# A fused attention and expert kernel: the first head's maxima moved ahead, and three smaller moves

## The chip, the cores and the metric
One core of a Trainium2 chip runs the whole program in one launch. The core has five engines that each work through their own list of instructions in order: TensorE (PE; its weight loads are shown as PEld), VectorE (DVE), ScalarE (ACT), GpSimd (POOL) and SyncE (SP), which here only starts transfers. ACT starts some transfers too, from the same list as its arithmetic. The metric is the device time of one execution in microseconds (us). Before the change it is 790.23 us, the median of three runs (789.36 to 791.34).

## The reference
Three steps follow each other. Only the first is touched by most of the change.

```python
# clustered attention: 2 batches x 8 heads, 768 tokens, head size 64, 16 centroids per head
q_assign = argmax(q_n @ c_n); k_assign = argmax(k_n @ c_n)         # rows normalised
mask   = q_assign[..., :, None] == k_assign[..., None, :]
scores = where(mask, q @ k.T / 8, -1e9); scores -= max(scores, -1)
attn   = exp(scores); attn /= sum(attn, -1) + 1e-9
x = (attn @ v) laid out as 1536 tokens x 512
# dense layer: 512 -> 2048 -> 512, weights arrive as 64-bit floats
x = (s * relu(x @ w_in) ** 2 + b) @ w_out
# 8 experts, top 1: logits from the rows of x and of expert_emb, both normalised
logits = xn @ en.T / tau; e = argmax(logits)
out = softmax(logits)[e] * (relu(x @ w1[e]) @ w2[e])
```

## The kernel before
The attention handles 16 heads one after the other, and the work of neighbouring heads is interleaved. A list of entries `(time, function)` is filled with `at(t, f)` and sorted by time; the functions are called in that order, and `order.pin` fixes each engine's list to it. A head is 12 units of this time long: head j starts at `o = 12 * j`, and the table `TIMES` gives each step's place against `o`. The numbers are only an order, not microseconds; in the steady part a head takes about 15 us.

For one head the steps are these. `load` fetches q, k and v. `split` cuts q and k into a rounded high part (ACT) and a rest (POOL; DVE for head 0). `trans` transposes them, three blocks of 128 columns at a time, in four calls: k first half, k second half, q first half, q second half. Each goes to a PSUM bank and ACT copies it to `kb` or `qb`; for all heads but the first, all four use the one bank `t`, so a transpose waits for the copy before it. `sims_mm` multiplies with the centroids; `sims_a` to `sims_e` and `masks`, all on DVE, turn that into one-hot rows scaled by 2^33, which are laid under the high parts of q and k in `qa` and `ka`. For heads 0 and 1 four copies do this, two on ACT and two on DVE; later heads use transfers. `M` then gives masked scores for 128 queries by 384 keys, and DVE takes their row maximum; there are 12 such pairs per head. `mneg` joins the maxima and negates them, `mrow` turns them into a row (a small matmul `mr`, an ACT copy `mrs`, a transfer into row 96 of `qa`). `Sx` computes the scores transposed, with the mask and the maximum already in the product, and ACT takes the exponential into `pt`; there are 12 per head too, in the two banks `s0` and `s1`. `V` multiplies `pt` with v into the bank `pv`, in three pairs of two (units 5.45, 9.45 and 13.45). `pv_out` reads that bank on ACT with two instructions, `vm` and `xu`, and the next head's first `V` may write it only after that. `sums` and `norm_a` to `norm_c` divide by the sums of the exponentials.

Head j's maxima and head j+2's or j+3's transposes stand among head j's neighbours' scores. Before head 0's first `Sx`, nothing but such preparation can run: heads 0 to 2 are split, transposed and masked there, and head 0's and half of head 1's maxima are taken. `cst.heat` issues matmuls on constant data whose result is not used; two follow each of head 0's 12 `M`. Head 0's `M` rotate over five PSUM banks, those of later heads over `M0` and `M1`.

`Moe.hooks` puts steps of the later layers into the same list. `fetch` and the last of nine steps of `conv_steps` start two transfers of 512 KB each on ACT's queue, for a raw weight tile pair (six buffers); the other eight steps convert an earlier pair from 64-bit floats, on ACT and DVE. `length`, `unit` and `project` prepare the expert embeddings: ACT sums squares, `unit` is eight DVE instructions, `project` is four transposes into bank `t` and one DVE instruction. They are used first in the routing after the dense layer's first 512 tokens.

Of the kernel before, what the change touches and what calls it, by code (L numbers as in the profile page):

```python
# [9 lines left out]
F32 = mybir.dt.float32  # L10
# [5 lines left out]
AF = mybir.ActivationFunctionType  # L16
# [5 lines left out]
P = 128  # L22
# [3 lines left out]
HS = S // 2  # L26
# [2 lines left out]
MASK = float(2 ** 33)  # L29
GUARD = 1e-9  # L30
TIMES = dict(load=-49, loadv=-18, split=(-42, -40), trans=(-36.6, -35.6, -33.6, -32.6), sims=-30.53, simv=(-26.5, -26.5, -26.5, -22.52, -22.52, -22.51),
             M=-17.4, mneg=-5.7, mrow=-3.5, V=(5.45, 5.45, 9.45, 9.45, 13.45, 13.45), presum=3.0, norm=(14.5, 25.47, 29.5, 29.5, 29.5))
ENDS = {14: (14.5, 21.47, 22.4, 23.4, 24.4), 15: (14.5, 14.6, 14.7, 14.8, 14.9)}
WARM = -26
HEAT = ((-41, 7), (-30.5, 6), (-22, 6))
SETUP, FETCH = 6.3, (5.3, 17.3, 29.3)
CONV = (3.2, 5.2, 7.2, 11.2, 15.2, 19.2, 23.2, 27.2, 31.2)
F, DM, TC = 2048, 512, 512
NF, KD, NTT = F // P, DM // P, TC // P
E, F2 = 8, 1024  # L40
# [51 lines left out]


def attention(ax, tc, cst, q, k, v, cen, xt, hooks, embed):
    nc = tc.nc
    ident, identr, ones, desc, cc, ps = cst.ident, cst.identr, cst.ones64, cst.desc, cst.cc, cst.ps
    io = ax.enter_context(tc.tile_pool(name="io", bufs=3))
    w1 = ax.enter_context(tc.tile_pool(name="w1", bufs=2))
# [5 lines left out]
    qa = [ab.tile([P, S], F32R, name=f"qa{i}") for i in range(NSET)]  # L104
    ka = [ab.tile([P, S], F32R, name=f"ka{i}") for i in range(NSET)]
# [66 lines left out]
    si, sm = {}, {}  # L172
# [31 lines left out]

    def masks(j):
        i = j % NSET
        ot = w1.tile([P, HS], F32, name="ot", tag="ot")
        nc.vector.transpose(out=ot, in_=si.pop(j))
        for g in range(4):
            da, w = (qa, ka)[g // 2][i], slice(g % 2 * HS, (g % 2 + 1) * HS)  # L210
            if j >= NSET:
                nc.sync.dma_start(out=da[64:64 + NC_, w].bitcast(F32), in_=ot[32 * g:32 * g + NC_])
            elif j > 1:
                nc.sync.dma_start(out=da[64:96, w].bitcast(F32), in_=ot[32 * g:32 * g + 32])
            elif g % 2 == 0:
                nc.scalar.activation(out=da[64:96, w], in_=ot[32 * g:32 * g + 32], func=AF.Copy)
            else:
                nc.vector.tensor_copy(da[64:96, w], ot[32 * g:32 * g + 32])

    def M(j, r, c):  # L220
        i = j % NSET
        pp = ps([P, HS], "M", f"M{c}" if j else ("M0", "M1", "s0", "s1", "s2")[(2 * r + c) % 5])
        nc.tensor.matmul(pp, qa[i][0:80, r * P:(r + 1) * P], ka[i][0:80, c * HS:(c + 1) * HS])  # L223
        nc.vector.tensor_reduce(out=mxt[j % 2][:, r, c:c + 1], in_=pp, axis=AX.X, op=ALU.max)  # L224
# [90 lines left out]
    c = w1.tile([P, D], F32, name="c", tag="c")  # L315
# [21 lines left out]
    def at(t, f, *a):  # L337
        ops.append((t, len(ops), f, a))
# [8 lines left out]
    T = TIMES  # L347
    for j in range(NH):
        o = 12 * j
        if j >= 3:  # L350
            at(o + T["load"], load, j, "qk")
            at(o + T["loadv"], load, j, "v")
        if j > 0:
            for i in range(2):
                at(o + T["split"][i], split, j, i)
        for i in range(4):
            at(o + T["trans"][i], trans, j, "kq"[i // 2], i % 2)
        at(o + T["sims"], sims_mm, j)
        for i, f in enumerate((sims_a, sims_b, sims_c, sims_d, sims_e, masks)):
            at(o + T["simv"][i], f, j)  # L360
        for r in range(NR):
            for c in range(2):
                at(o + T["M"] + 2 * r + c, M, j, r, c)
                if j == 0:
                    at(o + T["M"] + 2 * r + c, cst.heat, 2, "pv")
        at(o + T["mneg"], mneg, j)
        at(o + T["mrow"] if j else -5.6, mrow, j)
        for t in range(NR):
            for c in range(2):
                at(o + 2 * t + c, Sx, j, t, c)  # L370
            at(o + T["V"][t], V, j, t)
            at(o + 2 * t + T["presum"], presum, j, t)
        for i, f in enumerate((pv_out, sums, norm_a, norm_b, norm_c)):
            at(o + ENDS.get(j, T["norm"])[i], f, j)
# [6 lines left out]
class Moe:  # L381
# [11 lines left out]
    def hooks(self, ms, mb):  # L393
        nc = self.nc

        def early():
            for i, t in enumerate((ms, mb)):
                nc.sync.dma_start(out=self.sb[:, i:i + 1], in_=t.rearrange("(o n) -> o n", o=1).to_broadcast([P, 1]))
            self.setup()

        def fetch(f):
            self.loaded[f] = self.load_f64(f, nc.scalar)

        self.loaded, self.wT, self.wraw, self.running = {}, {}, {}, {}
        out = [(-27, self.length), (SETUP, early), (-16.6, self.unit), (SETUP + 9, self.project)] + [(t, lambda f=f: fetch(f)) for f, t in enumerate(FETCH)]
        for f in range(NWA):
            for n, t in enumerate(CONV):
                out.append((36 * f + 16 + t if f < NWA - 1 else 176.2 + n, lambda f=f: next(self.steps(f), None)))
        return out
# [50 lines left out]
    def ps(self, shape, name, tag):  # L460
        return self.cst.ps(shape, name, dict(a="pv", b="sm", y0="t", y1="s0", y2="s1", y3="s2").get(tag, tag))
# [124 lines left out]
    def moe1(self, xt):  # L586
# [4 lines left out]
        for c in range(self.chunks):  # L591
# [4 lines left out]
            def up(f):  # L596
# [4 lines left out]
                if final:  # L601
                    self.load_expert(f + 1)
                    if f in PRE0:
                        z = PRE0.index(f)
                        with self.after(*tail):
                            self.pre0[z] = self.half(self.wraw[0, z], 0, nc.gpsimd, False)
                hp = self.ps([P, TC], "hp", f"M{f % 2}")
                self.up_mm(hp, *wu, lambda k: x[k // 2][:, k % 2], lambda k: x[2 + k // 2][:, k % 2])
# [431 lines left out]
    def prep(self, xr):  # L1040
# [12 lines left out]
        return xh, xl  # L1053

    def block(self, y, args, w, pre, hooks, wd=None, g0=None):
        nc = self.nc
        xh, xl, off, _ = args
# [5 lines left out]
        def up(f):  # L1063
            with ExitStack() as behind:
# [5 lines left out]
                if f not in wd:  # L1070
                    wd[f] = self.half(w[f], 1, nc.vector)
            hp = self.ps([P, T], "hp", f"M{f % 2}")
            if xl is None:
# [79 lines left out]
@with_exitstack  # L1153
def tile_kernel(ctx, tc, q, k, v, cen, w_in, w_out, ms, mb, emb, tau, w1, w2, out):
    nc = tc.nc
    cst = consts(ctx, tc)
    xp = ctx.enter_context(tc.tile_pool(name="xp", bufs=1))
    xt = [xp.tile([P, KD, TC], F32, name="xt", tag=f"xt{i}") for i in range(NT // TC)]
    sb = cst.pool.tile([P, 2], F32, name="sb")
    moe = Moe(ctx, tc, cst, w_in, w_out, sb, emb, tau, w1, w2, out)  # L1160

    with ExitStack() as ax:
        attention(ax, tc, cst, q, k, v, cen, xt, moe.hooks(ms, mb), moe.embed)
    moe.pools()
    moe.xp = xp
    moe.moe1(xt)
    moe.spare = [xp.tile([P, KD, TC], dt, name="spare", tag=f"xt{i}") for i, dt in enumerate((F32R, F32R, F32))]
    moe.experts()
# [26 lines left out]
```

## Time and profile before

| | before |
|---|---|
| median of three runs | 790.23 us |
| profiled execution, its own time | 785.38 us |
| its span, first to last instruction | 783.5 us |
| mean granted TensorE clock | 0.987 of full |
| PE busy | 747.7 us, 95% |
| DVE busy | 518.4 us, 66% |
| ACT busy | 423.3 us, 54% |
| POOL busy | 352.1 us, 45% |

The profiled execution is one of many and has its own time, 4.85 us below the median; 1.88 us of it lie outside the span. Busy times are sums over the span. PE is busy nearly throughout, so what counts is where it is not, and whether its work there is of use: the matmuls of `heat` count as busy.

### The profile page before, as it was taken

What the parts mean: (1) busy time and instruction counts of PE and PEld (TensorE: products, weight loads), DVE (VectorE), ACT (ScalarE), POOL (GpSimd) and SP (SyncE); (2) the same over time, 40 slices, a digit from 0 to 9 for tenths busy, and PEclk for the clock granted to TensorE, in tenths of its full rate; (3) what the DMA queues carried; (4) which work ended last, traced back from release to release, by engine and by line L of the source; (5) the groups of instructions that cost most, each with busy time, mean ns of one, the idle gap of its engine ahead of it and who ended that gap; (6) DMA issues with size and microseconds to landing.
All of it is one profiled execution on the core that took longest, in us unless ns stands there. A gap on an engine that the chain in (4) does not pass through costs nothing. (4 is left out here: it accounts for less than half of the span.)

```text
span 783.5 us, 12256 instructions
## 1 busy us (share of the span) xinstructions
PE 747.7 (95%) x4193; PEld 564.0 (72%) x4193; DVE 518.4 (66%) x1100; ACT 423.3 (54%) x843; POOL 352.1 (45%) x282
## 2 busy tenths in 40 slices
PE   7799999999999899999999999999999999999993
PEld 3465555565555468888787887877879998988983
DVE  5768989797997889984354442557567365755750
ACT  5266555655554576555445564454557365755650
POOL 3166776676685565445333544467132302230001
PEclk9899999999999999999999999999999999999997
DMA  5145443434322225511000042265235555865600
GB/s 154 42 129 176 107 124 81 140 87 135 79 64 80 69 61 171 161 55 54 1 1 1 1 161 82 81 215 167 80 117 177 184 192 179 250 215 195 220 17 24
DMA packets 75678, 88.72 MB, mean 113 GB/s; under 512 B 7526, under 2 KB 58630, under 8 KB 75345
## 3 DMA queue, kind: packets, MB, share of 16 engines
q1 hardware_dynamic: 66688, 66.52, 28.1%
q0 software_dynamic: 4208, 13.90, 5.5%
q10 hardware_dynamic: 4704, 7.34, 2.8%
q8 instruction: 40, 0.66, 0.3%
q14 instruction: 38, 0.30, 0.1%
HBM read 70.57 MB, written 7.34 MB: 99 GB/s over the span
## 5 line engine op out<-in xcount | busy, mean ns | idle before, releaser
L534 POOL TENSOR_TENSOR wl<-w,wh 128x512 fp32r<-128x512 f32 x96 | 123.0, 1306 | 128.8 <-ACT wh L532 126.1
L249 ACT ACTIVATE pt<-S 128x384 f32<-128x384 f32 x192 | 91.8, 489 | 101.1 <-PE S L248 98.8
L224 DVE TENSOR_REDUCE mx<-M 128x1 f32<-128x384 f32 x192 | 101.9, 552 | 37.1 <-PE M L223 34.6
L260 POOL TENSOR_TENSOR acc<-acc,pt 128x768 f32<-128x768 f32 x61 | 106.0, 1737 | 5.7 <-ACT pt L249 3.3
L555 PE MATMUL hp<-x,wh 128*128 128x512 f32 x384 | 105.1, 395 | 0.3 <-ACT wh L532 0.3
L555 PE MATMUL hp<-x,spare 128*128 128x256 f32 x732 | 96.0, 284 | 2.0 <-PEq L987 1.7
L555 PEld LDWEIGHTS hp<-x,spare 128*128 128x128 f32 x732 | 92.6, 190 | 6.9 <-issue 4.1
L563 PE MATMUL y<-wd,gg 128*128 128x512 f32 x360 | 93.2, 394 | 0.0
L611 DVE SCALAR_TENSOR_TENSOR hp<-hp,sb,t 128x512 f32<-128x512 f32 x48 | 36.4, 758 | 74.6 <-ACT t L610 74.6
L223 PE MATMUL M<-ka,qa 80*128 80x384 f32 x192 | 79.0, 412 | 4.2 <-DVE mx L224 3.1
L555 PEld LDWEIGHTS hp<-x,wh 128*128 128x128 f32 x384 | 70.6, 188 | 15.1 <-ACT wh L532 0.9
L563 PE MATMUL y<-wh,gh 128*128 128x512 f32 x192 | 74.9, 390 | 0.0
L563 PE MATMUL y<-wl,gh 128*128 128x512 f32 x192 | 74.7, 389 | 0.0
L247 PE MATMUL S<-qa,ka 97*128 97x384 f32 x192 | 71.0, 370 | 2.1 <-ACT pt L249 1.4
L268 PE MATMUL pv<-pt,vn 128*64 128x385 f32 x384 | 72.8, 500 | 0.0
L548 DVE TENSOR_TENSOR wd<-w,wd 128x512 fp32r<-128x512 f32 x64 | 43.3, 686 | 44.1 <-ACT wd L547 43.3
L563 PEld LDWEIGHTS y<-wd,gg 128*128 128x128 f32 x360 | 63.8, 189 | 9.9
L1036 POOL DMA_INDIRECT row<-rows,idx x24 | 27.9, 1163 | 88.0 <-PE tp L1048 49.1
L248 PE MATMUL S<-qb,kb 128*128 128x384 f32 x192 | 65.5, 341 | 0.0
L610 ACT ACTIVATE t<-hp 128x512 f32<-128x512 f32 x48 | 28.7, 598 | 67.6 <-PE hp L555 67.5
L223 PEld LDWEIGHTS M<-ka,qa 80*128 80x128 f32 x192 | 36.9, 192 | 38.2 <-DVE su L296 8.1
L532 ACT ACTIVATE wh<-w 128x1024 fp32r<-128x1024 f32 x48 | 50.4, 1055 | 17.7 <-PE y L563 12.9
(275 smaller groups left out, 1352.2 us busy)
## 6 DMA issues: line engine op xcount, KB each, us to landing
w<-in_moe_w_dram SPq DMA_DIRECT2D x128, 256.0 KB
raw<-in_moe_w_in_dram SPq DMA_DIRECT2D x9, 512.0 KB
raw<-in_moe_w_out_dram SPq DMA_DIRECT2D x9, 512.0 KB
raw<-in_moe_w_in_dram ACTq DMA_DIRECT2D x7, 512.0 KB
raw<-in_moe_w_out_dram ACTq DMA_DIRECT2D x7, 512.0 KB
qn<-in_q_dram SPq DMA_DIRECT2D x16, 192.0 KB
kn<-in_k_dram SPq DMA_DIRECT2D x16, 192.0 KB
vn<-in_v_dram SPq DMA_DIRECT2D x16, 192.0 KB
```

Source lines behind the costliest of these rows:

```text
L223: nc.tensor.matmul(pp, qa[i][0:80, r * P:(r + 1) * P], ka[i][0:80, c * HS:(c + 1) * HS])
L224: nc.vector.tensor_reduce(out=mxt[j % 2][:, r, c:c + 1], in_=pp, axis=AX.X, op=ALU.max)
L247: nc.tensor.matmul(pp, ka[i][0:97, t * P:(t + 1) * P], qa[i][0:97, w], start=True, stop=False)
L248: nc.tensor.matmul(pp, kb[i][:, t * P:(t + 1) * P], qb[i][:, w], start=False, stop=True)
L249: exps.setdefault((j, t), []).append(nc.scalar.activation(out=p[:, c, 0:HS], in_=pp, func=AF.Exp, scale=0.125).ins)
L260: eng.tensor_tensor(out=acc[j][-1], in0=acc[j][-1], in1=p[:, :, 0:HS], op=ALU.add)
L268: together(tc, [lambda c=c: nc.tensor.matmul(pv_t[j][c * 64:c * 64 + 64, :], io_t["v", j][:, t, :], p[:, c, :], start=t == 0, stop=t == NR ...
L532: nc.scalar.activation(out=wh, in_=w, func=AF.Copy)
L534: eng.tensor_tensor(out=wl[:, a], in0=w[:, a], in1=wh[:, a].bitcast(F32), op=ALU.subtract)
L548: eng.tensor_tensor(out=t[:, 1], in0=w[:, a], in1=t[:, 0].bitcast(F32), op=ALU.subtract)
L555: self.nc.tensor.matmul(hp, a[:, k * P:(k + 1) * P], b(k), start=n == 0, stop=n == 3 * KD - 1)
L563: self.nc.tensor.matmul(y[i], (gl if n == 2 else gh)[:, s], wl if n == 1 else wh, start=first and n == 0, stop=last and n == 2)
```

## The change
Four things move. The diff is shown whole but for context.

```diff
-             M=-17.4, mneg=-5.7, mrow=-3.5, V=(...), presum=3.0, norm=(14.5, 25.47, 29.5, 29.5, 29.5))
+             M=(-17.4, 1), mneg=-5.7, mrow=-3.5, V=(...), presum=3.0, norm=(15.45, 25.47, 29.5, 29.5, 29.5))
-CONV = (3.2, 5.2, 7.2, 11.2, 15.2, 19.2, 23.2, 27.2, 31.2)
+CONV = (3.2, 5.2, 7.2, 11.2, 15.2, 19.2, 23.2, 27.2, 29.48)
     def masks(j):
-        ot = w1.tile([P, HS], F32, name="ot", tag="ot")
+        ot = sm[j] = w1.tile([P, HS], F32, name="ot", tag="ot")
...
-            elif g % 2 == 0:
-                nc.scalar.activation(out=da[64:96, w], in_=ot[32 * g:32 * g + 32], func=AF.Copy)
-            else:
+            elif g % 2:
                 nc.vector.tensor_copy(da[64:96, w], ot[32 * g:32 * g + 32])
+    def copies(j):
+        for g in (0, 2):
+            nc.scalar.activation(out=(qa, ka)[g // 2][j][64:96, 0:HS], in_=sm[j][32 * g:32 * g + 32], func=AF.Copy)
...
+        if j < 2:
+            at((-22.5, -8.5)[j], copies, j)
         for r in range(NR):
             for c in range(2):
-                at(o + T["M"] + 2 * r + c, M, j, r, c)
+                first, step = T["M"] if j else (-20.7, 0.95)
+                at(o + first + step * (2 * r + c), M, j, r, c)
                 if j == 0:
-                    at(o + T["M"] + 2 * r + c, cst.heat, 2, "pv")
-        at(o + T["mneg"], mneg, j)
-        at(o + T["mrow"] if j else -5.6, mrow, j)
+                    at(o + first + step * (2 * r + c), cst.heat, 1, "pv")
+        at(o + T["mneg"] if j else -9.9, mneg, j)
+        at(o + T["mrow"] if j else -9.8, mrow, j)
...
-        out = [(-27, self.length), (SETUP, early), (-16.6, self.unit), (SETUP + 9, self.project)] + [...]
+        out = [(-27, self.length), (SETUP, early), (49.5, self.unit), (53.4, self.project)] + [...]
```

The first place is PE's list where head 0's maxima begin. Here `qs` are head 1's q parts, `qb_117` and `kb_121` head 1's transposed q and k, `qa_108` and `ka_112` head 0's operands; `work` is what `heat` multiplies. Before:

```order
L162 MATMUL tp<-identr,qs 128x128 x6
L178 MATMUL si<-qb_117,cc 32x384 x2
L178 MATMUL si<-kb_121,cc 32x384 x2
L223 MATMUL M<-ka_112,qa_108 128x384
L1133 LDWEIGHTS work
L1133 MATMUL heat<-work 128x512
L1133 LDWEIGHTS work
L1133 MATMUL heat<-work 128x512
```

And the same place in the list of the changed kernel:

```order
L162 MATMUL tp<-identr,qs 128x128 x3
L225 MATMUL M<-ka_112,qa_108 128x384
L1138 LDWEIGHTS work
L1138 MATMUL heat<-work 128x512
L162 MATMUL tp<-identr,qs 128x128 x3
L225 MATMUL M<-ka_112,qa_108 128x384
L1138 LDWEIGHTS work
L1138 MATMUL heat<-work 128x512
L225 MATMUL M<-ka_112,qa_108 128x384
L1138 LDWEIGHTS work
L1138 MATMUL heat<-work 128x512
L178 MATMUL si<-qb_117,cc 32x384 x2
```

Three of the twelve maxima now stand ahead of head 1's products with the centroids, one of them between the two halves of head 1's q transposes, and one `heat` matmul follows each instead of two.

The second place is the end of head 0's maxima on PE, where its row `mr` is made. `qb_118` and `kb_122` are head 2's, `qa_109` and `ka_113` head 1's. Before, and behind it the changed list:

```order
L178 MATMUL si<-qb_118,cc 32x384 x2
L178 MATMUL si<-kb_122,cc 32x384 x2
L223 MATMUL M<-ka_112,qa_108 128x384
L1133 LDWEIGHTS work
L1133 MATMUL heat<-work 128x512
L1133 LDWEIGHTS work
L1133 MATMUL heat<-work 128x512
L235 MATMUL mr<-identr,mn 6x128
L223 MATMUL M<-ka_113,qa_109 128x384 x5
L162 MATMUL tp<-identr,ks 128x128 x3
```

```order
L225 MATMUL M<-ka_112,qa_108 128x384
L1138 LDWEIGHTS work
L1138 MATMUL heat<-work 128x512
L237 MATMUL mr<-identr,mn 6x128
L162 MATMUL tp<-identr,qs 128x128 x6
L178 MATMUL si<-qb_118,cc 32x384 x2
L178 MATMUL si<-kb_122,cc 32x384 x2
L225 MATMUL M<-ka_113,qa_109 128x384 x5
L162 MATMUL tp<-identr,ks 128x128 x3
```

The whole of head 2's q transposes and its products with the centroids moved from ahead of `mr` to behind it. On ACT the copies of head 1's masks moved too, from ahead of head 2's two `qb` copies to behind them; head 0's mask copies stand in ACT's list where they stood.

The third place is ACT's list in head 3, with that head's `pv_out` of head 2 (`vm`, `xu`) and the two weight transfers. Before, then changed:

```order
L168 ACTIVATE qb_118<-tp 128x384
L276 ACTIVATE vm<-pv 128x1
L277 ACTIVATE xu<-pv,vm 128x384
L249 ACTIVATE pt_127<-S 128x384
L168 ACTIVATE qb_118<-tp 128x384
L249 ACTIVATE pt_128<-S 128x384 x2
...
L249 ACTIVATE pt_131<-S 128x384 x2
L525 DMA raw<-in_moe_w_in_dram 128x4x256
L526 DMA raw<-in_moe_w_out_dram 128x1024
L168 ACTIVATE kb_123<-tp 128x384
```

```order
L168 ACTIVATE qb_118<-tp 128x384
L251 ACTIVATE pt_127<-S 128x384
L168 ACTIVATE qb_118<-tp 128x384
L278 ACTIVATE vm<-pv 128x1
L279 ACTIVATE xu<-pv,vm 128x384
L251 ACTIVATE pt_128<-S 128x384 x2
...
L530 DMA raw<-in_moe_w_in_dram 128x4x256
L531 DMA raw<-in_moe_w_out_dram 128x1024
L251 ACTIVATE pt_131<-S 128x384 x2
L168 ACTIVATE kb_123<-tp 128x384
```

`vm` and `xu` moved behind one exponential and the second `qb` copy, in this and every head that has them; the transfers moved ahead of two exponentials, four times in the attention.

## Rows read from the trace of the kernel before
**Rows 1.** Stretches: bounds, length, busy us (instructions) by engine, granted clock, DMA share, GB/s.
```profile
13.00:16.00 3.00, 1.52 (x13) 0.67 (x14) 0.00 (x0) 2.25 (x5) 0.51 (x1) 1.00 0.29 65
16.00:20.00 4.00, 4.00 (x13) 1.82 (x12) 3.48 (x13) 0.00 (x0) 1.44 (x2) 0.57 0.51 148
36.00:40.00 4.00, 3.48 (x13) 3.29 (x14) 2.77 (x7) 1.36 (x3) 0.00 (x0) 0.58 0.04 11
```
**Rows 2.** Timeline before head 0's scores: start, us, engine, line, operation [idle before <-releaser].
```profile
12.81 0.52 ACT L216 ACTIVATE ka<-ot 32x384 fp32r<-32x384 f32 x1
13.89 0.44 PE L162 MATMUL tp<-identr,qs 128*128 128x128 f32 x3 [1.09 <-ACT qb L168]
15.70 0.44 PE L223 MATMUL M<-ka,qa 80*128 80x384 f32 x1
16.25 0.56 DVE L224 TENSOR_REDUCE mx<-M 128x1 f32<-128x384 f32 x1 [3.25 <-PE M L223]
19.36 0.58 DVE L184 STREAM_TRANSPOSE si<-si 128x384 f32<-128x384 f32 x1
21.44 1.94 DVE L224 TENSOR_REDUCE mx<-M 128x1 f32<-128x384 f32 x4
23.30 0.36 DVE L199 TENSOR_TENSOR si<-si,smx 128x192 f32<-128x192 f32 x1
25.45 1.02 DVE L224 TENSOR_REDUCE mx<-M 128x1 f32<-128x384 f32 x2
26.32 0.57 PE L162 MATMUL tp<-identr,qs 128*128 128x128 f32 x3 [2.09 <-ACT qb L168]
29.35 0.73 PE L178 MATMUL si<-qb,cc 128*32 128x384 f32 x2
30.34 0.44 PE L223 MATMUL M<-ka,qa 80*128 80x384 f32 x1
31.41 0.17 DVE L230 TENSOR_REDUCE mn<-mx 128x6 fp32r<-128x18 f32 x1
31.74 0.59 PE L223 MATMUL M<-ka,qa 80*128 80x384 f32 x2
36.90 0.53 PE L247 MATMUL S<-qa,ka 97*128 97x384 f32 x1
```
**Rows 3.** Timeline of PE and ACT around one head's `pv_out`.
```profile
86.41 0.18 ACT L276 ACTIVATE vm<-pv 128x1 f32<-128x1 f32 x1
86.58 0.45 PE L162 MATMUL tp<-identr,qs 128*128 128x128 f32 x3 [0.20 <-ACT vm L276]
86.62 0.58 ACT L277 ACTIVATE xu<-pv,vm 128x384 f32<-128x384 f32 x1
87.10 0.49 ACT L249 ACTIVATE pt<-S 128x384 f32<-128x384 f32 x1
87.64 0.44 PE L247 MATMUL S<-qa,ka 97*128 97x384 f32 x1
88.18 1.51 PE L268 MATMUL pv<-pt,vn 128*64 128x385 f32 x8
```
**Rows 4.** Timeline of PE and ACT where weight transfers are started.
```profile
141.73 0.96 ACT L249 ACTIVATE pt<-S 128x384 f32<-128x384 f32 x2 [1.55 <-PE S L248]
142.74 0.46 ACTq L526 DMA_DIRECT2D raw<-in_moe_w_out_dram  x1
143.79 0.45 PE L162 MATMUL tp<-identr,ks 128*128 128x128 f32 x3 [0.48 <-ACT kb L168]
```
**Rows 5.** Timeline of ACT: `vm` in three other heads.
```profile
55.40 0.18 ACT L276 ACTIVATE vm<-pv 128x1 f32<-128x1 f32 x1
71.23 0.18 ACT L276 ACTIVATE vm<-pv 128x1 f32<-128x1 f32 x1
102.30 0.18 ACT L276 ACTIVATE vm<-pv 128x1 f32<-128x1 f32 x1
```
**Rows 6.** Timeline of PE: a late head without transposes.
```profile
240.78 0.45 PE L247 MATMUL S<-qa,ka 97*128 97x384 f32 x1 [0.25 <-ACT pt L249]
```

More of the change, by code (lines that the diff above doesn't have):

```diff
@@ L31 @@
 TIMES = dict(load=-49, loadv=-18, split=(-42, -40), trans=(-36.6, -35.6, -33.6, -32.6), sims=-30.53, simv=(-26.5, -26.5, -26.5, -22.52, -22.52, -22.51),
-             M=-17.4, mneg=-5.7, mrow=-3.5, V=(5.45, 5.45, 9.45, 9.45, 13.45, 13.45), presum=3.0, norm=(14.5, 25.47, 29.5, 29.5, 29.5))
+             M=(-17.4, 1), mneg=-5.7, mrow=-3.5, V=(5.45, 5.45, 9.45, 9.45, 13.45, 13.45), presum=3.0, norm=(15.45, 25.47, 29.5, 29.5, 29.5))
 ENDS = {14: (14.5, 21.47, 22.4, 23.4, 24.4), 15: (14.5, 14.6, 14.7, 14.8, 14.9)}
@@ L404, in hooks @@
         self.loaded, self.wT, self.wraw, self.running = {}, {}, {}, {}
-        out = [(-27, self.length), (SETUP, early), (-16.6, self.unit), (SETUP + 9, self.project)] + [(t, lambda f=f: fetch(f)) for f, t in enumerate(FETCH)]
+        out = [(-27, self.length), (SETUP, early), (49.5, self.unit), (53.4, self.project)] + [(t, lambda f=f: fetch(f)) for f, t in enumerate(FETCH)]
         for f in range(NWA):
```

## Prediction
> **What bounds the kernel now.** I read the page's busy times first: PE is busy for 95% of the span, so a change pays only where PE waits or does work that is not needed. Then the timeline of the first 37 us. There the reader should see that PE's share is high only because of the idle matmuls of `heat`, and that the work which must be done is a chain over DVE: head 0's twelve maxima, with head 1's mask steps in between, from 16.25 to the negation at 31.41 [rows 2]. Head 1's maxima follow at 31.74, and the first score matmul starts at 36.90 [rows 2]. Last I read PE's waits in the steady heads: they are few and short, about 0.2 us for a q transpose in each head [rows 3] and 0.48 where weight transfers are started [rows 4]. From the first score on the engines repeat one pattern, so I expect a shift of that point to arrive at the end whole.
>
> The granted clock has two levels here. [...]
>
> **Head 0's maxima, step by step.** The first `M` needs ACT's second mask copy, which ends at 12.81 + 0.52 = 13.33 [rows 2]. Its place on PE is now ahead of the second half of head 1's q transposes, so it can start at 13.38 instead of 15.70 [rows 2]. Those transposes wait for an ACT copy until 13.89 anyway [rows 2], so the `M` and its `heat` fit in front of them. From matmul to DVE takes 0.55 (15.70 to 16.25) [rows 2]: 13.93. DVE then has to do twelve maxima at 0.485 (1.94 for four), 5.8 us; head 1's first five mask steps, 2.1 (19.36 to 21.44); the rest of them with two copies, 2.15 (23.30 to 25.45); and the negation, 0.2 [rows 2]. For gaps I add 1.0: 0.1 because the first maximum stands alone (0.56), 0.3 before the second, whose `M` is behind the transposes of 13.89, and 0.6 before the fourth, whose `M` is behind head 1's products with the centroids (29.35 to 30.34, 1.0, for head 2's at the low clock; somewhat less at the high one) [rows 2]. The negation ends at about 13.93 + 5.8 + 2.1 + 2.15 + 0.2 + 1.0 = 25.2, against 31.41 + 0.17 = 31.58 [rows 2]. Two things pay for this: the early start (2.3), and DVE not standing still; the embedding's eight instructions are part of what lay between 16.81 and 19.36 beyond two maxima, about 1.55 [rows 2].
>
> **What is late next.** `mr` waits for the negation, and queued behind it on PE now are head 2's q transposes, its products, and head 1's maxima, which all stood or had their inputs ahead of it before. Counted from 25.2: `mr` 0.1, three transposes 0.57, their ACT copy 0.05 + 0.49 (a 128x384 pass, as the exponential of [rows 3]), the other three 0.05 + 0.57 because both use bank `t`, their copy 0.05 + 0.49, and then, on ACT, head 1's two mask copies at 0.52, while PE does the products in 1.0 [rows 2]. That makes 28.7 for head 1's first `M`, against 31.74 [rows 2]: of the 6.4 us 3.0 are left. PE has stood idle for some 5 us by then (its last `M` needs only a free bank, at about 20), so I took the low-clock durations. From that `M` to the first score 31.74 to 36.90, 5.16, went by in before [rows 2], set by two banks and DVE's mask steps of head 2; I add 0.3 for low-clock matmuls. First score at 34.2: **2.7 us gained**. The row's transfer has eight microseconds and is no limit.
>
> Bounds: if the clock is low at 16 to 20 too, a matmul of that mix takes 4.00 / 13 = 0.31 [rows 1], a pair of `M` and `heat` 0.62, 0.13 more than DVE's 0.485, for seven pairs 0.9; with 0.3 more later, 1.5 is the low end. With the high clock throughout, and no 0.6 gap, it is 2.7 + 0.3 + 0.3 + 0.6 = 3.9. I take 2.7, made of the rows of the same instructions.
>
> **The clock at the first scores.** PE waits as much in the 5 us ahead of them as before, so I leave the low stretch of 36 to 40 in place, at nothing. It may lie wholly before the scores or run on for another stretch: the score matmul there took 0.53 against 0.44 for a like one later [rows 2, 3], so about a fifth of some 3.3 us, 0.7 either way.
>
> [...]
>
> **Weight transfers.** In the fourth head `vm` comes 102.30 - 86.41 = 15.89 after the one before, against 86.41 - 71.23 = 15.18 in the third [rows 3, 5]. The difference is the head in which ACT starts two transfers: the k copy queues behind them, and PE waits for it, 0.48 [rows 4]. The changed list puts them ahead of two exponentials, before which ACT stood idle for 1.55 [rows 4]; two starts of about 0.46 [rows 4] fit in. The same happens three times with k transposes behind, the fourth time without any. **2.0 us gained** (3 x 0.7, less a little); ends: 0, if ACT's idle time there is needed, and 2.1.
>
> **Embeddings.** `project` stood between two transposes that use the same bank. The head with it took 71.23 - 55.40 = 15.83, 0.65 more than 15.18 [rows 3, 5]. At 53.4 it stands between the second q copy and head 4's `pv`, where bank `t` is free for six units, and costs at most what three larger transposes take, 0.45 [rows 3]; `unit` falls behind head 6's masks, where DVE has idle time. **0.4 gained**; ends 0 and 0.65.
>
> **`pv_out` one step later.** Take [rows 3]. In the changed list ACT does the exponential at 86.41, to 86.90; the second q copy starts when its transposes end, 86.58 + 0.45 = 87.03, and runs to 87.55; `vm` overlaps its end by 0.1 and starts at 87.45, `xu` 0.21 after that, 87.66, and ends at 88.24. `pv` can follow at 88.29. Before, it started at 88.18, behind a score matmul that had itself waited for the exponential (87.10 + 0.49 = 87.59, and the matmul at 87.64); without that wait PE would be at `pv` at 88.07. So `pv` is now held by `xu` and comes 0.11 later than before, in twelve heads: 1.3 us. Behind it on PE are the products for three heads on and the next `M`; on ACT two exponentials move by 0.7, whose banks are not needed until after `pv`'s 1.51 [rows 3]. In the two heads without transposes (12 and 13) the score matmul's wait of 0.25 [rows 6] goes: 0.5 back. **0.8 us lost.** Ends: 0.2 lost in each of twelve and nothing back, 2.4 lost; or `pv` not held at all and 0.11 gained in twelve, 1.3 + 0.5 = 1.8 gained.
>
> **Sum.** 2.7 + 0 + 2.0 + 0.4 - 0.8 = 4.3 us. The profiled execution's 785.38 would become 781.1; the median lies 4.85 above it, and I move it by the same: 790.2 - 4.3 = **785.9 us**.
>
> **Rivals.**
> 1. *The early start is spent again.* Head 1's maxima wait for head 2's transposes and the copies, as worked out, but each step comes later than I drew it, and the scores gain only about 1 us or less. For it: three engines hand over to each other nine times in that chain. Against it: every duration is taken at the low clock. Without the 2.7 the sum is 1.6, with 1.0 of it 2.6: around 788.
> [...]
> 3. *The `pv` bank decides, and the kernel is slower.* If the exponential does not start at `vm`'s old place, so that the q copy, `vm` and `xu` keep their distance to it, `xu` ends at 88.65 and `pv` starts at 88.70, 0.52 late; with the 0.1 that a stopped PE takes to resume (the 0.44 of [rows 3]) and the exponentials behind it, up to 0.7 in each of twelve heads, 8.4. The other terms bring 5.1, so it decides from 0.43 a head, and gives up to 793.5. Against it: ACT is free at 86.41, since `vm` starts there.
> 4. *All goes well*: high clock at the scores, `pv` not held: 3.3 + 0.7 + 2.1 + 0.6 + 1 = 7.7, 782.5.
> That the change does not do what it says holds for one part: head 0's mask copies keep their place in ACT's list, which costs or gains nothing.
>
> **Chances.** My forecast 0.58, rivals 1 and 2 together 0.24, rival 3 0.06, rival 4 0.12. The forecast's own range is 784 to 787.5; with most of rivals 1, 2 and 4 it becomes **782.8 to 788.8**. A measurement of this kernel tells about 0.3% from no change, 2.4 us, so the border is 787.8: faster has the forecast, rival 4 and a small part of the second, 0.75; the same has most of rivals 1 and 2 and a part of 3, 0.20; slower 0.05.
>
> **What would show it.** First `M` at about 13.4, negation at about 25, head 1's first `M` at 28 to 29, first score at 34 to 34.6; `vm` to `vm` 15.2 in the heads with weight transfers; `pv` in the steady heads waiting about 0.1 to 0.2 for `xu`, and those heads at about 15.3 rather than 15.18. The forecast is wrong if the first score comes after 35.5, or if steady heads take over 15.6.

## The result: slower, 801.76 us

The median went from 790.47 (789.36 to 791.34, six runs) to 801.76 us (799.23 to 804.65, six runs): a ratio of 1.0146, 95% interval 1.012 to 1.0173. The forecast was 785.9, a gain; its range ended at 788.8. The profiled execution took 802.95 us with a span of 801.1 and a mean granted clock of 0.970; before's had 785.38, 783.5 and 0.987.

**The early part went about as drawn.** ACT, PE and DVE in the timeline of the changed kernel, against [rows 2]:

```profile
12.75 0.52 ACT L220 ACTIVATE ka<-ot 32x384 fp32r<-32x384 f32 x1
13.32 0.44 PE L225 MATMUL M<-ka,qa 80*128 80x384 f32 x1 [0.59 <-ACT ka L220]
24.95 0.17 DVE L232 TENSOR_REDUCE mn<-mx 128x6 fp32r<-128x18 f32 x1
25.17 0.27 PE L237 MATMUL mr<-identr,mn 128*6 128x128 f32 x1 [4.28 <-DVE mn L232]
29.09 1.01 PE L225 MATMUL M<-ka,qa 80*128 80x384 f32 x2
34.88 0.52 PE L249 MATMUL S<-qa,ka 97*128 97x384 f32 x1
```

First `M` 13.32 (13.4 predicted), end of the negation 24.95 + 0.17 = 25.12 (25.2), head 1's first `M` 29.09 (28.7), first score 34.88 (34.2): 2.0 us earlier than in [rows 2]. The first steps end at another time in each execution, so to compare profiles I count from the end of ACT's second mask copy of head 0, which stands at the same place in both lists and ends at 13.2 to 15.5 in the profiles here: 12.75 + 0.52 = 13.27 in this one, 13.33 in [rows 2]. The first score comes 21.61 us after it, and 21.59 to 21.62 in six more profiles of kernels with this start; it was 23.57 in [rows 2]. But the first `vm` comes at 54.81, against 55.40 [rows 5], so only 0.6 of that was left 20 us later. The stretches of the changed kernel show why (columns as in [rows 1]):

```profile
16.00:20.00 4.00, 3.90 (x21) 2.31 (x21) 3.51 (x8) 0.49 (x1) 1.40 (x2) 1.00 0.52 145
20.00:25.00 5.00, 0.89 (x4) 0.30 (x3) 4.78 (x13) 0.49 (x1) 0.00 (x0) 0.78 0.18 39
25.00:30.00 5.00, 3.67 (x17) 1.65 (x17) 0.23 (x2) 3.23 (x7) 0.69 (x1) 0.50 0.24 50
30.00:36.00 6.00, 3.89 (x14) 2.85 (x14) 4.91 (x11) 0.73 (x2) 1.26 (x2) 0.50 0.17 61
36.00:40.00 4.00, 4.00 (x18) 3.78 (x18) 2.77 (x6) 2.42 (x7) 0.00 (x0) 0.52 0.27 61
```

PE is busy for 0.89 of the five microseconds from 20 to 25, and then the clock stays at its lower level until about 40. Before had it low in two shorter stretches there (0.66 from 25 to 30 below, 0.58 from 36 to 40 [rows 1]), and from 16 to 20, at 0.57 [rows 1], where the changed kernel has 1.00:

```profile
20.00:25.00 5.00, 4.23 (x25) 2.24 (x23) 4.79 (x12) 1.28 (x3) 0.00 (x0) 1.00 0.19 42
25.00:30.00 5.00, 3.68 (x17) 1.51 (x17) 2.54 (x6) 2.24 (x5) 0.99 (x1) 0.66 0.19 41
30.00:36.00 6.00, 3.46 (x20) 1.54 (x12) 4.26 (x11) 1.17 (x3) 0.99 (x1) 1.00 0.22 66
```

**The loss lies in the four heads that start weight transfers.** From one `vm` to the next a steady head takes 15.28 to 15.31 in the changed kernel, as predicted, and 15.44 with the embeddings; the four in question took 19.15, 20.31, 20.51 and 17.00. Before, the first of them took 15.89 [rows 3, 5] and the last 14.47. All waits of PE from 40 to 295 us that name the maximum row (engine, line, what it waited for: total us, times, longest), changed kernel, then before:

```profile
PE S L249 <- DMA qa<-mrs: 8.2, 5, 2.3
```

```profile
PE S L247 <- DMA qa<-mrs: 0.4, 1, 0.4
```

The first such head in the timeline of the changed kernel:

```profile
90.36 0.58 SPq L123 DMA_DIRECT2D vn<-in_v_dram  x1
91.31 0.39 ACTq L530 DMA_DIRECT2D raw<-in_moe_w_in_dram  x1
91.33 0.25 ACT L239 ACTIVATE mrs<-mr 6x128 f32<-6x128 f32 x1
91.60 0.75 SPq L240 DMA_DIRECT2D qa<-mrs  x1
91.79 0.47 ACTq L531 DMA_DIRECT2D raw<-in_moe_w_out_dram  x1
...
96.77 0.42 PE L249 MATMUL S<-qa,ka 97*128 97x384 f32 x1 [2.05 <-DMA qa<-mrs]
...
98.28 2.83 PE L270 MATMUL pv<-pt,vn 128*64 128x385 f32 x8
```

And the same place before, whose weight transfers start 2.4 us after the row and not 0.3 us ahead of it:

```profile
93.58 0.76 SPq L238 DMA_DIRECT2D qa<-mrs  x1
...
96.01 0.39 ACTq L525 DMA_DIRECT2D raw<-in_moe_w_in_dram  x1
96.49 0.50 ACTq L526 DMA_DIRECT2D raw<-in_moe_w_out_dram  x1
96.54 0.34 PE L247 MATMUL S<-qa,ka 97*128 97x384 f32 x1
```

The program leaves the row 96.54 - 93.58 = 2.96 us from its start to the next head's first score. Before, it lands in that time. Changed, the score comes 5.17 us after the start. Meanwhile the transfers move 372 GB/s, with all 16 DMA engines in use, and PE is busy for 0.82 of 3 us; then the clock falls:

```profile
94.00:97.00 3.00, 0.82 (x4) 0.44 (x3) 1.25 (x3) 0.84 (x2) 2.92 (x3) 1.00 0.99 372
97.00:98.00 1.00, 1.00 (x8) 0.82 (x7) 0.13 (x1) 0.53 (x2) 0.92 (x2) 0.92 0.14 52
98.00:101.00 3.00, 3.00 (x12) 1.11 (x12) 2.73 (x12) 0.83 (x2) 1.36 (x1) 0.50 0.33 71
```

`pv` takes 2.83 us at the lower level, against 1.51 [rows 3]. So a head loses twice: it waits for the row, 2.05, 2.20, 2.35 and, in the last, 1.18 us, and it loses another 1.8 to 2.9 us with PE at the lower level behind the wait. The fifth wait of the list above, 0.4, is the one that before has too.

Adding up the profiled executions: from the first `vm` to the last, 234.60 us against 220.36, 14.2 longer. The four heads are 3.9, 5.0, 5.2 and 3.0 longer than their like without weights, 17.1; before's excess of 0.7 in three of them is gone, 2.1; the rest is within 0.8. The whole span is 17.6 us longer: another 4.0 us come after the last `vm`, and 0.6 less before the first. What follows the last `vm` takes 507 to 513 us in the profiles of all kernels here, and goes with the chip and not with the change: 507.3 to 508.0 in the four kernels measured on one chip, 510.3 to 512.5 in the eight measured on two others. Before's 507.7 is a short one, so the medians' 11.3 us is the better figure.

### The profile page after: what moved, and what is told of

Same layout as the page of the kernel before. It is cut to its first block, busy times and chain, and to the rows that moved or that the text cites. A ratio compares the mean times of both kernels' runs of the same rounds, so it can differ in the third digit from the quotient of the medians.

```text
span 801.1 us, 12230 instructions
## 1 busy us (share of the span) xinstructions
PE 754.6 (94%) x4181; PEld 569.9 (71%) x4181; DVE 518.2 (65%) x1100; ACT 423.5 (53%) x843; POOL 352.3 (44%) x282
## 5 line engine op out<-in xcount | busy, mean ns | idle before, releaser
L270 PE MATMUL pv<-pt,vn 128*64 128x385 f32 x384 | 77.7, 528 | 1.4
L225 PEld LDWEIGHTS M<-ka,qa 80*128 80x128 f32 x192 | 37.3, 195 | 39.0 <-DVE mx L226 7.0
L615 ACT ACTIVATE t<-hp 128x512 f32<-128x512 f32 x48 | 28.7, 598 | 67.3 <-PE hp L560 67.2
L537 ACT ACTIVATE wh<-w 128x1024 fp32r<-128x1024 f32 x48 | 50.4, 1056 | 17.6 <-PE y L568 13.1
```

What stands on the lines that cost most here:

```text
L270: together(tc, [lambda c=c: nc.tensor.matmul(pv_t[j][c * 64:c * 64 + 64, :], io_t["v", j][:, t, :], p[:, c, :], start=t == 0, stop=t == NR ...
L537: nc.scalar.activation(out=wh, in_=w, func=AF.Copy)
```

## Experiments

Theory: the row is late because the weights' megabyte is started just ahead of it and beside it on another queue, and the wait lowers the clock. Rivals: another part of the change is at fault; ACT's time for starting the transfers is; or the wait alone is, without the clock. All ratios are to the kernel before on the same chip, whose median is 786.53, 790.48 or 789.61 us there; the quotients of the medians differ from them by up to 0.2%.

**Which part.** Each part alone on the kernel before, and the change without its weights part (`CONV`'s last entry).

```diff
# undo_loads, against the changed kernel
-CONV = (..., 27.2, 29.48)
+CONV = (..., 27.2, 31.2)
# only_loads, against the kernel before: the opposite. only_pv: norm=(15.45, ...). 
# only_prologue: maxima, one heat each, copies(). only_embed, against the kernel before:
-(-16.6, self.unit), (SETUP + 9, self.project)
+(49.5, self.unit), (53.4, self.project)
```

> The changed kernel with only the weight transfers back at 31.2. Theory (the transfers, started beside the maximum row's 3 KB, hold that row up in four heads, and PE's wait for it is followed by a low clock): no wait of S for the row in heads 4, 7, 10 and 13, about 789 us (the first score 2 us earlier, pv 0.1 us later in twelve heads, the k copy's wait of 0.5 back in three heads). Rival (pv held by xu costs the time): stays near 801.

> The kernel before with only the weight transfers moved to 29.48. Theory: S waits for the row, 2 us in each of four heads, a low clock behind it, so 12 to 13 us slower than before, about 803 us. Rivals (pv held by xu; half the heat matmuls): the transfers alone cost nothing, 788 to 790 us, as the prediction had it.

> The kernel before with only head 0's maxima moved ahead and half of the heat matmuls gone. If the first score's 2 us reach the end: a ratio of 0.9975. If the low clock at 20 to 42 us takes part of it back: 0.998 to 1.000, with the granted clock of that stretch below before's.

> The kernel before with only pv_out at 15.45. By the working of the prediction pv is held by xu 0.11 us in each of twelve heads and 0.5 us come back later: 0.8 us, a ratio of 1.001, heads of 15.28 instead of 15.18. If pv were the cause of the slow result: 1.01 or more.

> The kernel before with the embeddings' steps moved to head 4 alone. By the prediction 0.4 us gained (0 to 0.65). By the traces of the other runs, where head 4 took up to 1.1 us more: 0.3 to 0.5 lost. Either way within 0.997 to 1.002 of the kernel before, and only the heads' lengths in the trace can tell: head 1 shorter by 0.65, head 4 longer by 0.2 to 1.1.

| kernel | median us | before there | ratio | interval |
|---|---|---|---|---|
| without the weights part | 785.46 | 786.53 | 0.9985 | 0.9968 to 1.0002 |
| weights alone | 798.68 | 786.53 | 1.0173 | 1.0143 to 1.0203 |
| prologue alone | 790.51 | 790.48 | 0.9994 | 0.9977 to 1.001 |
| `pv_out` alone | 791.43 | 790.48 | 1.0004 | 0.9985 to 1.0023 |
| embeddings alone | 787.46 | 789.61 | 0.9969 | 0.9954 to 0.9985 |

The weights part alone gives the whole loss, with the same waits (6.5 us in five, the longest 2.1). The four single ratios multiply to 1.0140, and the whole change measured 1.0146; but their intervals together leave some 0.4%, 3 us, for parts that act on each other, and two of them do so ahead of the first score. The prologue kernel keeps the embeddings' eight DVE instructions among head 0's maxima, 1.5 us which the prediction's 25.2 had left out:

```profile
15.02 0.52 ACT L220 ACTIVATE ka<-ot 32x384 fp32r<-32x384 f32 x1
22.21 0.47 DVE L519 TENSOR_SCALAR emb<-emb,embn 8x512 f32<-8x512 f32 x1
40.16 0.52 PE L249 MATMUL S<-qa,ka 97*128 97x384 f32 x1
```

In its one profile, of the slowest of its runs, the first score comes 24.62 us after the mask copy, no earlier than with the old start (23.57 in before, 24.68 and 23.72 in the kernels with only the weights or only `pv_out` moved). With the embeddings alone it is 23.14, with both 21.6. So the prologue alone does not test the prediction's first term.

The embeddings' 0.9969 is more than the heads show: head 1 is 0.63 shorter, head 4 0.54 longer, and the first `vm` 0.5 earlier. That 0.5 is against the best of three profiles with the old start: counted from the mask copy the first `vm` comes after 41.64 us, against 42.07, 43.68 and 44.01. The rest may lie there; one profile of the kernel does not show it.

**Which property of the transfers.** Three kernels on the changed one: the same bytes later; the same bytes at the same place in the list, but on SP's queue, behind the row; and only the first half at the same place.

```diff
# loads_37
-CONV = (..., 27.2, 29.48)
+CONV = (..., 27.2, 37.3)
# loads_sp
-self.load_f64(f + 3, nc.scalar if f < NWA - 1 else nc.sync)
+self.load_f64(f + 3, nc.sync)
# half_loads: CONV = (..., 27.2, 29.48, 37.3), w_in at the first, w_out at the second
+            eng.dma_start(out=r[0]..., in_=self.wi[...])
+            yield
+            eng.dma_start(out=r[1]..., in_=self.wo[g])
```

> The changed kernel with the weight transfers at 37.3, the place in a head where the first three pairs are fetched, six units after the k transposes. Theory: the 1 MB is through before the next row is sent, and no k copy queues behind it, so no wait of S for the row and none of the k transposes: about 787 us. If the bytes in flight rather than the row's neighbourhood are the cause, S waits again somewhere and it stays above 795.

> The changed kernel with the four weight transfers at 29.48 started on SP's queue, in which the row stands ahead of them. Theory in its form that the row is late because weight packets of another queue are in front of it: the row is first and lands in time, no wait of S, 787 to 789 us. In the form that 1 MB in flight slows every small transfer, whatever the order: S still waits about 2 us in four heads, near 801.

> The changed kernel, but of the two 512 KB transfers only the first starts at 29.48; the second is a step of its own at 37.3. Theory (the maximum row's 3 KB wait for the bytes started just ahead of and beside it): with one transfer in flight the row lands some 1.3 us earlier (512 KB at 400 GB/s), so the waits of 2.05 to 2.35 us at the first score of the next head shrink to about 1 us or less, at times nothing; the clock falls in none or one of the three heads; 0.997 to 1.005 of the kernel before. Rival (the row waits because ACT's start of transfers holds it up, or because any large transfer at that place is enough): waits stay at 2 us and the ratio stays at 1.012 or more.

Later: 784.44 us, 0.9965 (0.9948 to 0.9983). The first three weights heads take 15.28 or 15.29, where the changed kernel with the old place has 15.93 to 15.95: the 2.0 us that the prediction hoped for are there, at this place. On SP: 784.98, 0.9985 (0.9972 to 0.9999), no wait for a row but the 0.4 us that before has too. Half: 792.17, 1.0021 (1.0006 to 1.0036), and in the timeline of that kernel

```profile
91.70 0.39 ACTq L451 DMA_DIRECT2D raw<-in_moe_w_in_dram  x1
91.97 0.76 SPq L240 DMA_DIRECT2D qa<-mrs  x1
...
96.25 0.42 PE L249 MATMUL S<-qa,ka 97*128 97x384 f32 x1 [1.15 <-DMA qa<-mrs]
...
143.37 0.41 PE L249 MATMUL S<-qa,ka 97*128 97x384 f32 x1 [0.94 <-DMA qa<-mrs]
...
190.31 0.50 PE L249 MATMUL S<-qa,ka 97*128 97x384 f32 x1 [0.90 <-DMA qa<-mrs]
```

Half the bytes, half the wait: the score comes 4.28 us after the row's start instead of 5.17. The clock fell after the third of these waits alone, to 0.50 from 191 to 193 us; after the other two it stayed at 1.00 (97 to 101, 147 to 151). What was started ahead of the row on the other queue delayed it here, and twice the bytes delayed it more. The kernel with SP's queue clears the bytes as such and the place in the list:

```profile
91.67 0.76 SPq L240 DMA_DIRECT2D qa<-mrs  x1
92.47 0.43 SPq L530 DMA_DIRECT2D raw<-in_moe_w_in_dram  x1
...
94.62 0.34 PE L249 MATMUL S<-qa,ka 97*128 97x384 f32 x1
```

The score comes 2.95 us after the row's start, without a wait. But the weights now start 0.80 us behind the row and not 0.29 ahead of it, and from 92 to 93 us the DMA engines' share is 0.32, against 0.73 in the changed kernel; their 385 to 415 GB/s come from 95 to 98, behind the score. So whether the order within the queue or the later start saves the row is not shown. ACT's own time for starting them was no cost: `mrs` starts 0.18 us behind `pv` with the two starts on ACT and without them (91.33 after 91.15, 91.39 after 91.21), and the k copy behind them was not late in these heads.

In the changed kernel the 16 DMA engines' share is 0.99 from 94 to 97 us, while transfers of both queues are under way, and the row lands only as the stream ends: the score that waited for it starts at 96.77, and from 97 to 98 the share is 0.14. How the bytes on the other queue hold the row up no run here tells.

The kernel with SP's queue lost its gain elsewhere, in head 4 (19.41 us), where the embeddings stand. This is that head there:

```profile
101.03 0.44 PE L225 MATMUL M<-ka,qa 80*128 80x384 f32 x1 [0.73 <-DVE mx L226]
```

Its stretches from 98 to 108 us:

```profile
98.00:101.00 3.00, 2.10 (x14) 1.56 (x12) 2.86 (x7) 1.89 (x6) 2.18 (x2) 1.00 0.22 63
101.00:104.00 3.00, 2.97 (x12) 2.23 (x14) 2.03 (x5) 1.49 (x3) 1.23 (x1) 0.58 0.33 74
104.00:108.00 4.00, 4.00 (x17) 1.05 (x14) 1.84 (x5) 0.00 (x0) 0.00 (x0) 0.50 0.14 32
```

The eight DVE instructions hold up the maxima, PE waits 0.73 us for them, and with the low clock behind it the head is 4.1 us longer. With the transfers at 37.3 the same wait (0.75) was not followed by a low clock (1.00 from 101 to 108 us), and the head took 16.37. Why they hold up the maxima here and not in the changed kernel, one of the eight and its neighbour on GpSimd show, on SP's queue and then in the changed kernel:

```profile
96.00 3.44 POOL L262 TENSOR_TENSOR acc<-acc,pt 128x768 f32<-128x768 f32 x2
97.84 1.62 DVE L88 TENSOR_TENSOR embn<-embn 8x1 f32<-8x1 f32 x1
```

```profile
97.68 1.68 POOL L262 TENSOR_TENSOR acc<-acc,pt 128x768 f32<-128x768 f32 x1
100.01 0.15 DVE L88 TENSOR_TENSOR embn<-embn 8x1 f32<-8x1 f32 x1
```

This DVE instruction works on 8 elements. Where GpSimd was at work when it started, it took 1.62 us, on SP's queue, and 1.64 with the transfers at 37.3, and ended within 0.02 us of GpSimd's; in the changed kernel, where GpSimd had ended before, it took 0.15. The head goes with it: 0.1 to 0.2 us longer than its like at 0.15, 1.1 at 1.64, and 4.1 at 1.62, where the low clock followed.

**The clock's share of the loss.** On the changed kernel, nine idle matmuls ahead of each score that waits:

```diff
# wait_heat
+    for f in range(4):
+        at(36 * f + 47.95, cst.heat, 9, "s2")
```

> The changed kernel with nine idle matmuls (1.9 us at the high clock) put on PE ahead of the first score of heads 4, 7, 10 and 13, into the wait for the row. Theory (2.0 to 2.35 us of each such head are the wait, the other 1.9 to 2.9 us the low clock that follows it): the row is as late as before, the clock stays high behind it, and the kernel loses about 5 to 8 us over before instead of 12: a ratio of 1.006 to 1.010. Rival (the clock plays no part; the transfers still hold other things up afterwards): a ratio of 1.014 as for the whole change.

795.85 us against 790.48, 1.0051 (1.0036 to 1.0067), a little under the range expected. The row is about as late as in the changed kernel (92.80 to 97.69, 4.89 us, against 5.17), but the clock stays up:

```profile
94.00:97.00 3.00, 2.78 (x15) 1.94 (x16) 2.38 (x6) 1.34 (x3) 3.00 (x3) 1.00 0.94 325
97.00:98.00 1.00, 1.00 (x7) 0.54 (x5) 0.00 (x0) 0.00 (x0) 0.92 (x2) 1.00 0.99 369
98.00:101.00 3.00, 3.00 (x20) 1.51 (x18) 2.08 (x8) 1.26 (x3) 2.48 (x2) 1.00 0.28 71
```

The heads take 17.25, 17.74, 17.69 and 15.96. So of the 1.46% about 0.95 was the clock after the wait by the ratios, 5.9 of 11.3 us by the medians, and 8.3 of 17.1 us in the profiled heads; the remainder is about the wait. The rival without the clock falls.

**Putting it together.** First `loads_37` with idle matmuls in the prologue's waits; then a kernel with the late transfers at 37.3, the early ones on SP's queue behind head 2's masks, and the embeddings where DVE stands still after head 0's row; and last that kernel with the idle matmuls.

```diff
# loads_37_heat, and again in best
+    at(-9.85, cst.heat, 18, "pv")
+    at(-1.0, cst.heat, 6, "pv")
# best_b and best, on loads_37
-(49.5, self.unit), (53.4, self.project)
+(-9.0, self.unit), (17.4, self.project)
-            self.loaded[f] = self.load_f64(f, nc.scalar)
+            self.loaded[f] = self.load_f64(f, nc.sync)
```

> The changed kernel with the transfers at 37.3, and 18 idle matmuls ahead of mr and 6 ahead of head 1's sixth maximum, where PE stands idle. If the low clock before and at the first scores costs what I think, they start 0.5 to 1 us earlier and run at the high clock: a ratio of 0.993 to 0.995 against before, below the 0.9965 of the same kernel without them. If not, 0.9965 or, should the matmuls be in the way, more.

> The changed kernel with the late pair of transfers at 37.3, the three early pairs on the queue of SyncE instead of ScalarE's, the embeddings' eight DVE instructions right behind head 0's row, where DVE has nothing to do, and their product in head 1. Theory: the head with the embeddings loses its 1.1 us, no row and no mask transfer waits beside weights on another queue, and the early start of the scores is kept: 0.994 to 0.997 of the kernel before. Rival (the gain of the early start goes back to the clock whatever is done later): 0.997 to 0.9985, as with the late pair moved alone (0.9965), with the first 45 us holding as many low-clock stretches as there.

> As the kernel with early pairs on SyncE's queue, and with 18 idle matmuls ahead of head 0's row and six in head 1's maxima. Theory on the clock: PE's wait ahead of head 1's maxima is what lowers the clock at the first scores; with it filled the granted clock from 25 to 45 us stays above 0.9 and the time is 1.5 to 3 us under that kernel's, about 0.991 to 0.994 of the kernel before. Rival: the idle matmuls hold up the copies and transposes behind them as much as the clock returns, and the two kernels differ by under 1 us.

The first, expected at 0.993 to 0.995, was no better than without: 788.91, 0.9973 (0.9954 to 0.9991). Its scores start at 34.70, but then the early weights, on ACT's queue since 39.86, delay head 2's masks on SP's, the same collision at another place, with a low clock behind it:

```profile
39.27 1.22 SPq L214 DMA_DIRECT2D ka<-ot  x2
39.86 0.45 ACTq L532 DMA_DIRECT2D raw<-in_moe_w_in_dram  x1
...
44.78 0.42 PE L225 MATMUL M<-ka,qa 80*128 80x384 f32 x1 [1.49 <-DMA ka<-ot]
```

Of the two mask transfers the first was started 0.6 us ahead of the weights here and the second beside them. In the changed kernel the first has 1.35 us (39.73 to 41.08), and nothing waits for it; so being first by 0.6 us was not enough here. The other two: 786.53, 0.9958 (0.9938 to 0.9978), and 785.33, 0.9943 (0.9923 to 0.9962), the lowest ratio of all, though not clear of 0.9965. Both have the fourth to the twelfth head at 15.26 to 15.31. Their first scores come at 34.82 and 34.80, but the first `vm` at 55.16 and 53.77. The stretches of the last show what lies between:

```profile
20.00:25.00 5.00, 4.84 (x24) 2.30 (x24) 4.78 (x13) 0.74 (x2) 0.00 (x0) 1.00 0.19 43
25.00:30.00 5.00, 3.21 (x21) 1.30 (x19) 2.44 (x12) 3.17 (x7) 0.28 (x1) 1.00 0.17 36
30.00:36.00 6.00, 5.67 (x20) 3.11 (x21) 4.72 (x11) 1.19 (x4) 1.68 (x2) 0.72 0.21 70
36.00:40.00 4.00, 3.69 (x23) 2.85 (x23) 3.75 (x8) 3.25 (x8) 1.70 (x1) 1.00 0.31 71
```

With PE kept busy from 20 to 25, the clock is up from 25 to 30 and from 36 to 40 and at 0.72 between, where the changed kernel had 0.50 to 0.52. The traces give 1.4 us for it at the first `vm`, or 2.2 counted from the mask copy (41.95 and 39.73 us); the two medians differ by 1.2, and their intervals overlap, so the gain in time is not shown.

## Why the prediction was wrong, step by step

- **Weight transfers, "2.0 us gained": the step that failed.** It asked whether ACT had time for two starts and whose copy stood behind them. Both were right: the k copy's wait went, 2.1 us. It did not ask what the megabyte would run beside. The new place lies next to `mrs` in ACT's list, and SP starts the row then. The sum called the row's transfer no limit because of its eight microseconds, which hold for head 0; in the steady heads it has 2.96, and both rows for that stood in the trace. The row then took 4.7 to 5.3 us from its start to the score that waited for it, and the low clock followed. Measured for this part alone: 1.0173, 12 to 14 us lost.
- **Start of the scores, 2.7 gained.** The chain was right to 0.4 us up to head 1's first `M`; the first score came 0.7 later than drawn, and 2.0 arrived there.
- **"The clock at the first scores", nothing, 0.7 either way.** Mis-sized: by these two profiles about 1.4 us lost between the first score and the first `vm`, with the clock at 0.50 to 0.52 from 25 to 40 us. From 25 to 36 us PE is busy about as long as before (7.56 against 7.14 us), as the prediction said, but with half the idle matmuls the 5 us ahead of `mr` were nearly empty (0.89 against 4.23). What the early start is worth by itself no kernel measures; the change without its weights part is at 0.9985 (0.9968 to 1.0002).
- **Embeddings, 0.4 gained.** By the heads' lengths in the changed kernel 0.55 gained and 0.14 lost: right, but by luck of where GpSimd's work fell. "Where DVE has idle time" did not ask what GpSimd does there; in other kernels that head lost up to 1.1 us, and 4.1 with the low clock behind it, which the bound of "0" had not allowed for. Alone the step measured better than that, 0.9969.
- **`pv_out`, 0.8 lost.** Steady heads cost 0.10 each, 0.11 predicted; `pv` waits for `xu` and the third rival did not happen. In the last heads more came back than the 0.5 expected: 14.00, 12.99 and 11.59 in the kernel with this step alone against 14.47, 13.13 and 12.51, 1.5 us. Alone it measured 1.0004, no difference.

None of the rivals had the row in it, so the chance of 0.05 for slower stood on the wrong mechanism.

## What to carry to other kernels

Before a large transfer is moved, list what other queues start in the microseconds around its new place, and for each small one read the time from its start to its first reader: that is its slack, and here a megabyte started just ahead of it took 1.2 to 2.4 us more than that. Put the large transfer where no reader is near, or behind the small one on the same queue, which here also started it about 1 us later. And price a new wait of a busy TensorE with the slow stretch that may follow it, which here was about as dear as the wait (1.8 to 2.9 us behind waits of 1.2 to 2.4).

## What the runs showed that I had not expected

- A 3 KB transfer took 4.7 to 5.3 us to its reader beside 1 MB started around it on another queue, and at most 2.95 in the head shown, with that megabyte started 0.80 us behind it on its own.
- The length of a wait did not tell whether the clock would fall: after waits of 1.15 and 0.94 us it stayed at 1.00, after one of 0.90 in the same kernel it fell to 0.50 (191 to 193 us).
- Nine idle matmuls in each wait for the row kept the clock at 1.00 (94 to 101 us) and took about 0.95% off the time by the ratios.
- A DVE instruction on 8 elements took 0.15 us where GpSimd had ended before it, and 1.62 and 1.64 where GpSimd was at work, until the GpSimd instruction beside it ended.
